# A fifth buffer of probabilities, one output staging tile less, and the exponential listed ahead of the copies in even slots

## The chip, the core and the metric

The kernel runs on one core of a Trainium2 chip. The core has five engines that each work through a queue of their own, in order: TensorE (PE in the profile; its weight loads are shown as PEld), VectorE (DVE), ScalarE (ACT), GpSimd (POOL) and SyncE (SP, which here only issues DMAs). They meet through semaphores. The metric is the time of one execution on the device, in microseconds (us), as the median of several runs.

## What is computed

Four batches of eight attention heads, 768 positions, 64 channels a head. A key counts for a query only if both fall into the same bucket of a hash of six sign bits. The heads of a batch, side by side, are the input of a gated convolution and two matrix products.

```python
def _attn_ref(q, k, v, proj):
    q_bits = (np.einsum('bhsd,dk->bhsk', q, proj) > 0)
    k_bits = (np.einsum('bhsd,dk->bhsk', k, proj) > 0)
    ...
    scores = scale * np.matmul(q, k.transpose(0, 1, 3, 2))
    scores = np.where(mask, scores, -1000000000.0)
    scores = scores - np.max(scores, axis=-1, keepdims=True)
    attn = np.exp(scores)
    attn = attn / (np.sum(attn, axis=-1, keepdims=True) + 1e-09)
    return np.matmul(attn, v)

def _moe_ref(x, w_val, conv_w, w_out):
    ...
    gate = 1.0 / (1.0 + np.exp(-gate_pre))
    val = x @ w_val
    return (gate * val @ w_out)
```

Here `gate_pre` is a causal convolution of five taps along the positions, each channel for itself.

## The kernel before

A **unit** is one head of one batch: 32 units. Each is cut into six query tiles of 128 rows, so there are 192 tiles, and one loop runs over **slots** k, with one tile entering the pipeline per slot. The order of the work on PE, DVE, ACT and POOL is the order of the program text: the schedule is written by hand, and each engine's queue is in order. What a slot k lists, engine by engine:

- **PE**: `scores(k + 1)` (four matrix products, L291, into one of two PSUM tiles `s`), then four matrix products of the feed-forward part (`moe`, L424 or L449) where a batch is ready for it, in odd slots two steps of `attn_v` (L362, into the tile `av`), and at the end `transposes(k - 3)`: six transpositions of 128x128 of the probabilities `p` of tile k-3 (L339), three into each of two PSUM tiles `tp`.
- **ACT**: `keep_transposed(k - 4)`, two copies (L348) that bring the two `tp` tiles of the previous slot's transpositions to SBUF (`pt`), then `exponentials(k)`, one exponential of 128x768 (L315) from `s` into a tile `p`, with the row sum accumulated. After that come, in some slots, an output copy (L457) or the two copies of a finished `av` into `x` (L370). A unit's `attn_v` begins three slots after its last tile and takes three odd slots, so its `x` copies stand at the end of an odd slot, once in every six slots, and the next slot, an even one, follows them in ACT's queue.
- **DVE**: the row maximum `nm` (L297), in even slots the row sums of the tiles k-2 and k-1 (L321), the scale `gs` (L303), in even slots the reciprocals (L325), the bias `nb` (L307) on which the exponential waits; then parts of the convolution (`g`, L393), the gate product `ht` (L429) and roundings.
- **POOL**: `normalise(k - 2)`, which multiplies `p` by the reciprocal (L330), and subtractions that split numbers into two parts.
- **SP**: the loads, the DMAs that rearrange a unit's operands, and the output DMAs (L459).

Four buffers matter for what follows. `s` has two, so `scores(k + 2)` waits for `exponentials(k)`. `tp` has two tiles, so the two halves of `transposes(k - 3)` wait for the two copies of `keep_transposed(k - 4)`. `p` has `LAG + 1 = 4` tiles, so `exponentials(k)` writes the tile from which `transposes(k - 4)`, of slot k-1, has read. The staging tile of an output, `o`, has two.

`outp` ends an output tile of 128x512: accumulated in PSUM, copied to `o` by DVE or ACT, sent out by a DMA on SP's queue. The last slots (k from 192 on) hold no scores, and after the loop the rest of the feed-forward part runs with `cur["end"]` set.

Of the kernel before, what the change touches and what calls it, by code (L numbers as in the profile page):

```python
# [8 lines left out]
FP32 = mybir.dt.float32  # L9
# [17 lines left out]
def kernel(  # L27
# [12 lines left out]
    P = 128  # L40
    D = 64
    KB = S // P
    HS = S // 2
    NP = H // 2
    KW = 5
    LAG = 3
# [5 lines left out]
    raw = ctx.enter_context(tc.tile_pool(name="raw", bufs=5))  # L52
    stk = ctx.enter_context(tc.tile_pool(name="stk", bufs=2))
    vp = ctx.enter_context(tc.tile_pool(name="vp", bufs=2))
    pp = ctx.enter_context(tc.tile_pool(name="pp", bufs=LAG + 1))
    small = ctx.enter_context(tc.tile_pool(name="small", bufs=6))
    ptp = ctx.enter_context(tc.tile_pool(name="ptp", bufs=6))
    xp = ctx.enter_context(tc.tile_pool(name="xp", bufs=2))
# [1 line left out]
    gp = ctx.enter_context(tc.tile_pool(name="gp", bufs=5))  # L60
    hp = ctx.enter_context(tc.tile_pool(name="hp", bufs=5))
    wst = ctx.enter_context(tc.tile_pool(name="wst", bufs=2))
    op = ctx.enter_context(tc.tile_pool(name="op", bufs=2))

    dram = ctx.enter_context(tc.tile_pool(name="dram", bufs=4, space=bass.MemoryType.DRAM))
    ps_s = ctx.enter_context(tc.tile_pool(name="ps_s", bufs=2, space=PSUM))
# [192 lines left out]
    def first_bits():  # L259
        yield from bits(0)  # L260
        load_raw(5)
# [47 lines left out]
    def exponentials(k):  # L309
        s, nb = ss.pop(k), nbs.pop(k)  # L310
        p = pp.tile([P, 2, HS], FP32, name="p")
        if k % 2 == 0:
            cur["sm"] = small.tile([P, 2, 2], FP32, name="sm")
        sm = cur["sm"]
        nc.scalar.activation(out=p, in_=s[:, :, 0:HS], func=AF.Exp, bias=nb, scale=gs.pop(k), accum_out=sm[:, k % 2, 0:1])  # L315
        ps[k] = (p.rearrange("p a b -> p (a b)"), sm)
# [25 lines left out]
    def keep_transposed(k):  # L342
        i, qt = tiles[k]
        if qt % 3 == 0:
            cur["pts"].append([ptp.tile([P, 3, HS], FP32, name="pt") for _ in range(2)])
        qo = (qt % 3) * P
        for pt, tp in zip(cur["pts"][-1], tps.pop(k)):
            nc.scalar.copy(out=pt[:, :, qo:qo + P], in_=tp[:, 0:HS].rearrange("p (a b) -> p a b", b=P))  # L348
        if qt == KB - 1:
            avs.append(attn_v(i, cur["pts"]))  # L350
            cur["pts"] = []

    def attn_v(i, pts):
        b, h = units[i]
        hh, c = h % 2, h // 2
        av = ps_v.tile([P, 512], FP32, name="av")
        vt = vts[i]
        for kb in range(KB):
            if kb:
                yield  # L360
            for s, pt in enumerate(pts):
                nc.tensor.matmul(out=av[s * D:(s + 1) * D, 0:HS], lhsT=vt[:, kb, hh * D:(hh + 1) * D], rhs=pt[kb // 3][:, kb % 3, :],  # L362
                                 start=(kb == 0), stop=(kb == KB - 1), tile_position=(0, s * D))
        if hh == 0:
            x = cur["x"] = xp.tile([P, S + KW - 1], FP32, name="x")
            nc.gpsimd.memset(x[:, 0:KW - 1], 0.0)
        x = cur["x"]
        for s in range(2):
            o = KW - 1 + s * HS
            nc.scalar.copy(out=x[hh * D:(hh + 1) * D, o:o + HS], in_=av[s * D:(s + 1) * D, 0:HS])  # L370
        if hh == 1:
            if c == 0:
                cur["xs"], cur["g"] = {}, []
            convs.append(pair_x(b, c, x, cur["g"], cur["xs"]))
# [34 lines left out]
    def moe(b, xs_, g):  # L409
        hs = {}  # L410
        todo = []

        def later():
            while todo:
                todo.pop(0)()

        def val(o, j):
            acc = acc_tile()
            m = 0
            for wi, xi in ((0, 0), (1, 0), (0, 1)):  # L420
                if m:
                    yield
                for c in range(NP):
                    nc.tensor.matmul(out=acc[:, 0:HS], lhsT=wv[wi][:, c, j * P:(j + 1) * P],  # L424
                                     rhs=xs_[(c, o)][xi], start=(m == 0), stop=(m == 11))
                    m += 1
                later()
            ht = hp.tile([P, HS], FP32, name="ht", bufs=2)
            nc.vector.tensor_tensor(out=ht, in0=acc[:, 0:HS], in1=g[j][:, o:o + HS], op=ALU.mult)  # L429

            def split():
                hh = hp.tile([P, HS], FP32R, name="hh")
                nc.vector.tensor_copy(out=hh, in_=ht)  # L433
                hl = hp.tile([P, HS], FP32R, name="hl")
                nc.gpsimd.tensor_tensor(out=hl, in0=ht, in1=hh.bitcast(FP32), op=ALU.subtract)  # L435
                hs[(o, j)] = (hh, hl)
            todo.append(split)
            yield

        def outp(o, tb):  # L440
            for gens in weights:
                finish(gens)
            acc = acc_tile()
            m = 0
            for hi, wi in ((0, 0), (0, 1), (1, 0)):
                if m:
                    yield
                for j in range(NP):
                    nc.tensor.matmul(out=acc, lhsT=hs[(o, j)][hi][:, tb * P:(tb + 1) * P],  # L449
                                     rhs=wo[wi][:, j, :], start=(m == 0), stop=(m == 11))  # L450
                    m += 1
                later()
            ob = op.tile([P, 512], FP32, name="o")
            if cur["gates"]:
                nc.vector.tensor_copy(out=ob, in_=acc)
            else:
                nc.scalar.copy(out=ob, in_=acc)  # L457
            r0 = o + tb * P
            nc.sync.dma_start(out=out[b, r0:r0 + P, :], in_=ob)  # L459
            yield  # L460

        def idle(n):
            for _ in range(n):
                later()
                yield

        def hold():
            while len(moes) < 2 and not cur["end"]:
                yield

        chunks = [(val, 0, j) for j in range(NP)]
        chunks += [(val, HS, 0)] + [(outp, 0, tb) for tb in range(3)] + [(val, HS, j) for j in range(1, NP)]
        chunks += [(idle, 2)] + [(outp, HS, tb) for tb in range(3)]
        if b < B - 1:
            chunks.insert(-2, (hold,))
        for f, *args in chunks:
            yield from f(*args)
# [5 lines left out]
    raws, stacks, vts, ss, nbs, ps, tps, sums, rcs, nms, gs, cur = {}, {}, {}, {}, {}, {}, {}, {}, {}, {}, {}, {}  # L483
# [11 lines left out]
    def finish(gens):  # L495
        while gens:
            step(gens)

    cur["gates"], cur["end"], cur["pts"] = 0, False, []
    N = len(tiles)  # L500
    with tc.manual_schedule(engines=ENGINES):
        for i in range(5):
            load_raw(i)
        load_values(0)
        first_prep()
        weights = [[load_weights()], [load_conv()]]
        preps = [first_bits(), prep(1)]
        scores(0)
        next(preps[1])
        step(preps)  # L510
        step(weights[0])
        step(weights[1])
        ahead = [early_bits()]
        for k in range(N + LAG + 1):
            if 0 <= k - LAG - 1:
                keep_transposed(k - LAG - 1)
            pair = k % 2 == 0 and 0 <= k - 2 < N
            if k < N:
                maxima(k)
            if pair:  # L520
                row_sums(k - 2)
            if k < N:
                factors(k)
            if pair:
                recip(k - 2)
            if 0 <= k - 2 < N:
                normalise(k - 2)
            if k < N:
                shifts(k)
            if k + 1 < N:  # L530
                if tiles[k + 1][0] != tiles[k][0]:
                    finish(preps)
                    preps = [prep(tiles[k + 1][0] + 1)]
                scores(k + 1)
            if k < N:
                exponentials(k)
            if k >= 60 or k % 2:
                step(convs)
            if k % 6 in (0, 2, 4, 5) and k > 4:
                step(weights[0])  # L540
            elif k < 6:
                step(weights[1])

            thin = k // 6 % 8 in (7, 0) and k < 186
            for _ in range(3 if cur["gates"] else (1, 0)[k % 2] if thin else 1):
                step(moes)
            cur["gates"] = max(0, cur["gates"] - 1)
            step(preps)
            if 6 <= k < 60 and k % 6 in (3, 4):
                step(ahead)  # L550
            if k % 2:
                step(avs)
                step(avs)
            if 0 <= k - LAG < N:
                transposes(k - LAG)
        accs[:] = [(ps_m, "m"), (ps_t, "tp"), (ps_s, "s"), (ps_t, "tp"), (ps_s, "s")]
        finish(avs)
        cur["gates"] = 0
        cur["end"] = True
        while convs:  # L560
            step(convs)
            step(moes)
        finish(moes)
# [59 lines left out]
```

## Time and profile before

| | us |
|---|---|
| median of 3 runs | 621.56 (620.15 to 621.71) |
| the profiled execution, its own time | 621.24 |
| its span, first to last instruction | 619.2 |
| ACT copies of L348, 384 of them | 165.7 |
| POOL busy | 387.6 |
| granted TensorE clock over the span | 0.997 |

The profile is of one execution; its page gives the busy time of every engine, the span in 40 slices, the chain of work that ended last, and the costliest groups of instructions. In a group's row stand the line of the kernel, the engine, the operation, what it writes and reads, how often it ran, its busy time and the mean of one, and then the idle time of the engine just before, with what ended most of it. In a row of the timeline stand the start and the length in us, the engine, the line, the operation, the tiles, and how many instructions are merged in the row; idle time before it is in brackets with its releaser. Matrix products are pipelined: the recorded end of one lies about a quarter of a microsecond behind the start of the next.

### The profile page before, as it was taken

The page shows a single profiled execution, that of the slowest core. Times are in us where ns is not written, and L with a number is a line of the kernel's source. Part 1 is how long each engine was busy: PE and PEld are TensorE (multiplying, and loading weights), DVE is VectorE, ACT ScalarE, POOL GpSimd, SP SyncE. Part 2 cuts the span into 40 slices and gives each one's busy share as a digit, 9 for nine tenths or more (in the row PEclk, how much of TensorE's full clock was granted, in tenths as well). Part 3 has the DMA queues.
Part 4 walks back from the last instruction along what each step waited for, and adds up shares of the span by engine and source line. Part 5 has one row for each costly group of instructions (what it writes and reads, how often), then busy time and mean ns, then how long its engine had stood idle before and what let it go on. Part 6 is the DMA issues. An engine that isn't in the chain of part 4 may idle for free.

```text
span 619.2 us, 10665 instructions
## 1 busy us (share of the span) xinstructions
PE 585.0 (94%) x3496; PEld 421.4 (68%) x3496; DVE 434.5 (70%) x1017; ACT 420.3 (68%) x881; POOL 387.6 (63%) x373
## 2 busy tenths in 40 slices
PE   5799998989899999999999999999999999999997
PEld 2665655556567776776668787777667777775895
DVE  5787889898885866668575867668665877665532
ACT  2786777677778676777787676777787766765400
POOL 3575777677866765578665777468764776544321
PEclk9899999999999999999999999999999999999999
DMA  7575767473533334243434234333422213200111
GB/s 228 167 209 168 216 170 208 129 202 82 132 82 74 79 77 130 73 108 83 125 80 115 55 83 123 87 112 83 108 70 78 68 43 92 66 19 1 51 52 51
DMA packets 29030, 64.64 MB, mean 104 GB/s; under 512 B 4936, under 2 KB 10056, under 8 KB 28976
## 3 DMA queue, kind: packets, MB, share of 16 engines
q1 hardware_dynamic: 28832, 63.93, 37.7%
q8 instruction: 28, 0.46, 0.3%
q14 instruction: 26, 0.21, 0.1%
q10 hardware_dynamic: 144, 0.03, 0.0%
HBM read 30.60 MB, written 7.86 MB: 62 GB/s over the span
## 4 chain that ended last, share of the span: by engine, by line
PE 71%; ACT 14%; DVE 11%; issue 2%; DMA 2%; SPq 0%; POOL 0%; ACTq 0%; DVEq 0%; POOLq 0%
PE av L362 19%; PE s L291 17%; PE tp L339 13%; PE m L449 8%; PE m L424 7%; ACT p L315 6%; ACT pt L348 4%; DVE nm L297 3%; ACT x L370 2%; DVE g L393 2%; PE tp L424 1%; PE tp L449 1%; PE s L449 1%; PE m L229 1%; PE s L424 1%
## 5 line engine op out<-in xcount | busy, mean ns | idle before, releaser
L330 POOL TENSOR_SCALAR p<-p,ri 128x768 f32<-128x768 f32 x192 | 205.0, 1072 | 157.7 <-DVE nb L307 131.3
L297 DVE TENSOR_REDUCE nm<-s 128x1 f32<-128x768 f32 x192 | 182.6, 951 | 63.9 <-PE s L291 63.5
L348 ACT COPY pt<-tp 128x384 f32<-128x384 f32 x384 | 165.7, 485 | 81.7 <-PE tp L339 80.9
L315 ACT ACTIVATE p<-s,nb,gs 128x768 f32<-128x768 f32 x192 | 192.7, 1003 | 40.5 <-DVE nb L307 35.6
L339 PEld LDWEIGHTS tp<-ident,p 128*128 128x128 f32 x1152 | 129.2, 141 | 71.8 <-issue 45.2
L339 PE MATMUL tp<-ident,p 128*128 128x128 f32 x1152 | 163.8, 278 | 2.8 <-ACT pt L348 2.2
L362 PE MATMUL av<-pt,vt 128*64 128x384 f32 x768 | 144.9, 498 | 0.0
L291 PE MATMUL s<-ak,aq 76*128 76x384 f32 x384 | 117.7, 387 | 19.6 <-ACT p L315 16.9
L291 PE MATMUL s<-bk,bq 128*128 128x384 f32 x384 | 100.6, 343 | 0.4 <-DVE bq L277 0.4
L362 PEld LDWEIGHTS av<-pt,vt 128*64 128x64 f32 x768 | 46.9, 136 | 63.0 <-issue 62.9
L291 PEld LDWEIGHTS s<-ak,aq 76*128 76x128 f32 x384 | 59.0, 193 | 35.6 <-ACT p L315 31.8
L393 DVE SCALAR_TENSOR_TENSOR g<-x,cw_sb,g 128x768 f32<-128x768 f32 x64 | 77.3, 1208 | 2.2 <-POOL g L391 2.1
L291 PEld LDWEIGHTS s<-bk,bq 128*128 128x128 f32 x384 | 71.2, 192 | 0.8 <-issue 0.8
L198 POOL TENSOR_TENSOR bq<-r,aq 128x768 fp32r<-128x768 f32 x31 | 57.5, 1853 | 0.1
L435 POOL TENSOR_TENSOR hl<-ht,hh 128x384 fp32r<-128x384 f32 x32 | 32.2, 1006 | 39.4 <-DVE hh L433 39.4
L370 ACT COPY x<-av 64x384 f32<-64x384 f32 x64 | 30.4, 474 | 30.9 <-PE av L362 30.2
L383 POOL TENSOR_TENSOR xl<-x,xh 128x384 fp32r<-128x384 f32 x32 | 33.4, 1059 | 18.0 <-DVE xh L382 18.0
L424 PE MATMUL m<-xh,wv 128*128 128x384 f32 x200 | 42.7, 337 | 0.0
L307 DVE TENSOR_SCALAR nb<-nm,gs 128x1 f32<-128x1 f32 x192 | 40.2, 209 | 3.5
L315 ACT ACTIVATION_READ_ACCUMULATOR p<-s,nb,gs 128x1 f32 x192 | 39.1, 203 | 0.0
L429 DVE TENSOR_TENSOR ht<-m,g 128x384 f32<-128x384 f32 x25 | 13.9, 556 | 35.7 <-PE m L424 29.3
L449 PE MATMUL m<-wo,hh 128*128 128x512 f32 x144 | 38.1, 394 | 0.0
(86 smaller groups left out, 483.7 us busy)
## 6 DMA issues: line engine op xcount, KB each, us to landing
r<-in_qk_dram SPq DMA_DIRECT2D x32, 384.0 KB
vt<-in_v_dram SPq DMA_DIRECT2D x16, 384.0 KB
out_dram<-o SPq DMA_DIRECT2D x24, 256.0 KB
ak<-aq SPq DMA_DIRECT2D x31, 192.0 KB
bk<-aq SPq DMA_DIRECT2D x31, 192.0 KB
bk<-bq SPq DMA_DIRECT2D x31, 192.0 KB
bq<-aq SPq DMA_DIRECT2D x31, 192.0 KB
hh<-in_qk_dram SPq DMA_DIRECT2D x16, 192.0 KB
```

What stands on the lines that cost most here:

```text
L198: nc.gpsimd.tensor_tensor(out=bq, in0=r, in1=aq.bitcast(FP32), op=ALU.subtract)
L291: nc.tensor.matmul(out=s[:, hf, 0:HS], lhsT=lq[0:n, qs], rhs=rk[0:n, hf * HS:(hf + 1) * HS], start=n == M, stop=n == P)
L297: nc.vector.tensor_reduce(out=nm, in_=s[:, :, 0:HS], axis=AX.XY, op=ALU.max, negate=True)
L315: nc.scalar.activation(out=p, in_=s[:, :, 0:HS], func=AF.Exp, bias=nb, scale=gs.pop(k), accum_out=sm[:, k % 2, 0:1])
L330: nc.gpsimd.tensor_scalar(out=p, in0=p, scalar1=rcs.pop(k), scalar2=1.0, op0=ALU.mult, op1=ALU.mult)
L339: nc.tensor.transpose(out=tp[:, n * P:(n + 1) * P], in_=p[:, kb * P:(kb + 1) * P], identity=ident)
L348: nc.scalar.copy(out=pt[:, :, qo:qo + P], in_=tp[:, 0:HS].rearrange("p (a b) -> p a b", b=P))
L362: nc.tensor.matmul(out=av[s * D:(s + 1) * D, 0:HS], lhsT=vt[:, kb, hh * D:(hh + 1) * D], rhs=pt[kb // 3][:, kb % 3, :], start=(kb == 0), s ...
L370: nc.scalar.copy(out=x[hh * D:(hh + 1) * D, o:o + HS], in_=av[s * D:(s + 1) * D, 0:HS])
L393: nc.vector.scalar_tensor_tensor(out=g, in0=x[:, k:k + S], scalar=w, in1=g, op0=ALU.mult, op1=ALU.add)
L424: nc.tensor.matmul(out=acc[:, 0:HS], lhsT=wv[wi][:, c, j * P:(j + 1) * P], rhs=xs_[(c, o)][xi], start=(m == 0), stop=(m == 11))
L449: nc.tensor.matmul(out=acc, lhsT=hs[(o, j)][hi][:, tb * P:(tb + 1) * P], rhs=wo[wi][:, j, :], start=(m == 0), stop=(m == 11))
```

## The change

Three edits. The ring of probabilities gets a fifth buffer. The staging tile `o` has one buffer in place of two, and after the loop the outputs are staged in the ring `p`, which is then free. In even slots below N = 192, `keep_transposed(k - 4)` is no longer listed at the head of the slot but behind `exponentials(k)`; odd slots, and those from 192 on, are as before.

```diff
-    pp = ctx.enter_context(tc.tile_pool(name="pp", bufs=LAG + 1))
+    pp = ctx.enter_context(tc.tile_pool(name="pp", bufs=LAG + 2))
...
-    op = ctx.enter_context(tc.tile_pool(name="op", bufs=2))
+    op = ctx.enter_context(tc.tile_pool(name="op", bufs=1))
...
-            ob = op.tile([P, 512], FP32, name="o")
+            if cur["end"]:
+                ob = pp.tile([P, 2, HS], FP32, name="p").rearrange("p a b -> p (a b)")[:, 0:512]
+            else:
+                ob = op.tile([P, 512], FP32, name="o")
...
         for k in range(N + LAG + 1):
-            if 0 <= k - LAG - 1:
+            if 0 <= k - LAG - 1 and (k % 2 or k >= N):
                 keep_transposed(k - LAG - 1)
...
             if k < N:
                 exponentials(k)
+                if k % 2 == 0 and 0 <= k - LAG - 1:
+                    keep_transposed(k - LAG - 1)
```

## The prediction, made before the change was run

> **What bounds the kernel now.** I read the page's busy times first, then the table of windows, the list of waits and the timeline.
>
> ```profile
> span 619.2 us, 10665 instructions
> PE 585.0 (94%) x3496; PEld 421.4 (68%) x3496; DVE 434.5 (70%) x1017; ACT 420.3 (68%) x881; POOL 387.6 (63%) x373
> PE 71%; ACT 14%; DVE 11%; issue 2%; DMA 2%; SPq 0%; POOL 0%; ACTq 0%; DVEq 0%; POOLq 0%
> ```
>
> PE carries the kernel: 94% busy and 71% of the chain that ended last. The windows (length, then busy time of PE, PEld, DVE, ACT, POOL) show where it isn't full:
>
> ```profile
> 10.10:193.00 182.90, 165.54 (x1026) 106.31 (x1026) 152.78 (x363) 136.37 (x290) 123.06 (x120) 0.99 0.56 155
> 193.00:557.10 364.10, 359.00 (x2166) 267.50 (x2165) 250.73 (x604) 266.32 (x562) 240.82 (x228) 1.00 0.33 85
> ```
>
> From 193 us on, PE idles 364.1 - 359.0 = 5.1 us in all, so nothing that frees another engine can gain more there. Before 193 us it idles 17.4 us, and DVE is busy 84% of that time. The waits name the causes (total, times, longest):
>
> ```profile
> ACT pt L348 <- PE tp L339: 80.9, 96, 2.1
> ACT p L315 <- DVE nb L307: 35.6, 45, 6.0
> PE s L291 <- ACT p L315: 16.9, 34, 2.0
> PE tp L339 <- ACT pt L348: 2.2, 7, 0.8
> ```
>
> ACT waits 80.9 us, 96 times, for transpositions that its next copies need. ACT isn't the bound, so that idle time costs nothing by itself. What costs is PE waiting for an exponential that frees an s tile: 16.9 us. That, with the 2.2 us for copies, is all that an order of ACT's queue could win.
>
> **The change part by part.** The reorder comes first. In an even slot ACT had the two copies, then the exponential; now the exponential, then the copies. No instruction is added. ACT's queue issues no DMA here, and neither SP's nor POOL's queue is moved past. But PE needs both: the copies free the tp tiles for the next transpositions, the exponential frees the s tile for the scores after these. The transpositions are listed first, so the copies are needed first.
>
> Slot A, behind x copies (one in six slots), with ACT's rows, PE's, the weight load of the scores and the bias:
>
> ```profile
> 409.27 0.97 ACT L370 COPY x<-av 64x384 f32<-64x384 f32 x2 [0.64 <-PE av L362]
> 410.27 0.86 ACT L348 COPY pt<-tp 128x384 f32<-128x384 f32 x2
> 411.02 1.01 ACT L315 ACTIVATE p<-s,nb,gs 128x768 f32<-128x768 f32 x1
> ```
>
> ```profile
> 409.15 0.87 PE L339 MATMUL tp<-ident,p 128*128 128x128 f32 x6
> ...
> 411.26 0.81 PE L339 MATMUL tp<-ident,p 128*128 128x128 f32 x6
> 412.17 0.62 PE L291 MATMUL s<-ak,aq 76*128 76x384 f32 x2
> ```
>
> ```profile
> 412.17 0.30 PEld L291 LDWEIGHTS s<-ak,aq 76*128 76x128 f32 x2 [0.33 <-ACT p L315]
> ```
>
> ```profile
> 409.00 0.21 DVE L307 TENSOR_SCALAR nb<-nm,gs 128x1 f32<-128x1 f32 x1
> ```
>
> The bias is there at 409.21, the x copies hold ACT until 410.24. Copies at 410.27, exponential at 411.02, transpositions at 411.26 without a stall, scores at 412.17 after a weight-load wait of 0.33 for the exponential. With the order turned I need three steps from rows elsewhere: how soon copies follow an exponential, a stalled transposition its copy, and scores their transpositions. Another x slot, in which PE had no feed-forward work:
>
> ```profile
> 458.50 0.86 ACT L348 COPY pt<-tp 128x384 f32<-128x384 f32 x2
> 459.24 1.01 ACT L315 ACTIVATE p<-s,nb,gs 128x768 f32<-128x768 f32 x1
> ...
> 460.23 0.48 ACT L348 COPY pt<-tp 128x384 f32<-128x384 f32 x1
> ```
>
> ```profile
> 459.12 0.85 PE L339 MATMUL tp<-ident,p 128*128 128x128 f32 x6
> ```
>
> Exponential to copies: 460.23 - 459.24 = 0.99. Copies to stalled transpositions: 459.12 - 458.50 = 0.62. So in slot A: exponential at 410.27, copies 411.26, transpositions 411.88 in place of 411.26, their end 0.85 later, 412.73. Scores may start 0.25 before that recorded end (slot B below: 352.25 + 0.82 against 352.82), at 412.48 in place of 412.17. The stall for the exponential goes, and a longer one for the copies takes its place: **0.3 us lost**.
>
> Slot B, without x copies but with a late bias (PE's rows, then the bias, then the next bias and its exponential):
>
> ```profile
> 350.12 0.88 PE L339 MATMUL tp<-ident,p 128*128 128x128 f32 x6
> ...
> 352.25 0.82 PE L339 MATMUL tp<-ident,p 128*128 128x128 f32 x6
> 352.82 0.60 PE L291 MATMUL s<-ak,aq 76*128 76x384 f32 x2
> ```
>
> ```profile
> 351.02 0.19 DVE L307 TENSOR_SCALAR nb<-nm,gs 128x1 f32<-128x1 f32 x1
> ```
>
> ```profile
> 353.55 0.21 DVE L307 TENSOR_SCALAR nb<-nm,gs 128x1 f32<-128x1 f32 x1
> ```
>
> ```profile
> 353.86 0.99 ACT L315 ACTIVATE p<-s,nb,gs 128x768 f32<-128x768 f32 x1 [0.22 <-DVE nb L307]
> ```
>
> Bias end to exponential is 353.86 - 353.76 = 0.10. The bias of slot B ends at 351.21, so the exponential starts at 351.31, copies 352.30, transpositions 352.92, end 353.77, scores 353.52: **0.70 us later** than 352.82, where PE had no wait before. This is an added wait: the copies are queued behind an exponential that waits for DVE, the transpositions wait for the copies, and behind these stand the next scores, since PE's queue is in order.
>
> The general rule from these steps: scores come 0.99 + 0.62 + 0.85 - 0.25 = 2.21 us after the exponential's start. Where neither x copies nor bias hold the exponential past about 0.45 us after the start of the transpositions, that is no later than before (2.7 us), and nothing is lost or won.
>
> I applied this to the 93 even slots from k = 4 to 188, each against the scores' start in the trace. 30 follow x copies. In 28 of them the turn costs at least 0.30: **8.4 us**, firm (in the other two PE waits longer for something else). In nine of them the bias comes later still, 4.1 us more. Of the 63 others, 32 lose by a late bias, 17.8 us in all; the first and the last:
>
> ```profile
> 22.25 0.21 DVE L307 TENSOR_SCALAR nb<-nm,gs 128x1 f32<-128x1 f32 x1
> ```
>
> ```profile
> 491.62 0.19 DVE L307 TENSOR_SCALAR nb<-nm,gs 128x1 f32<-128x1 f32 x1
> ```
>
> So the late biases sum to 21.9 us, but not all is paid. Two slots after B the bias is late again, because DVE has worked without a pause since before B:
>
> ```profile
> 357.40 0.21 DVE L307 TENSOR_SCALAR nb<-nm,gs 128x1 f32<-128x1 f32 x1
> ```
>
> That slot was counted at 0.77 beyond its x copies. If slot B has already put PE back 0.70, DVE has caught up and the 0.77 nearly vanishes. A run of late slots pays about once, and before 193 us, where most late slots lie (13.2 of the 17.8), DVE is nearly the bound. Where the bias is late because a gate product waited for PE, the loss stays. Bounds: 0 (all absorbed) and 21.9 (none). The nearest rows are those of B and its follower, where 0.70 of 0.70 + 0.77 is paid, 48%; I take half, **11.0 us**.
>
> The fifth p buffer costs no time: ACT's copies already waited for the transpositions that release the fourth, so it alone frees nothing; it is what lets the exponential go first. One staging tile: the next output copy must wait for the DMA. The closest pair in the loop, and the last output:
>
> ```profile
> 324.26 0.36 SPq L459 DMA_DIRECT2D out_dram<-o  x1
> ```
>
> ```profile
> 329.26 0.69 DVE L455 COPY o<-m 128x512 f32<-128x512 f32 x1 [3.72 <-PE m L449]
> ```
>
> ```profile
> 613.28 3.08 SPq L459 DMA_DIRECT2D out_dram<-o  x2
> ```
>
> 5.0 us lie between issue and next copy. The second of the last two is issued at about 616.0 (613.28 + 3.08 less 0.3), and the span ends 3.2 us later, landing included. So the wait has passed. If a landing took twice 3.2 us, two such pairs would cost 1.4 us each; at the other end nothing, and no gain, since nothing waited. I take 0. After the loop outputs follow every 2.75 us; two tiles sufficed (5.5 against 3.2), so a ring of five wins nothing.
>
> Sum: 8.4 + 11.0 = 19.4 us, none of it hidden, as PE is the bound. Against the profiled execution's own 621.24 us (span 619.2, 2.0 around it; 0.3 below the median of 621.56) that gives **640.6 us**.
>
> **The rivals.**
>
> *Only the x slots pay.* DVE catches up everywhere: 621.2 + 8.4 = 629.6. For it: DVE's idle time elsewhere. Against: biases that are late behind a gate product move with PE.
>
> *Everything pays.* 621.2 + 8.4 + 21.9 = 651.5. For it: odd exponentials also start later (their copies follow the delayed transpositions), so row sums and the next bias can be late again. Against: the run after slot B.
>
> *The other side, faster: the copies come in time.* The place is the even slot's second transposition, the price the 16.9 us that PE now waits for exponentials. It decides when the exponential starts within 0.45 us of the transpositions' start. Then the wait goes and nothing replaces it: 604.3, or 612.8 if half. Slot A speaks against it, as x copies end at +1.1 us.
> [...]
>
> *No difference*: losses and regained waits cancel, 621.2.
>
> **How the numbers follow.** Forecast (640.6, give or take 6) 0.43; x slots alone 0.27; everything 0.15; faster 0.09; no difference 0.06. The range reaches from 626, a little under the x slots alone, to 653, a little over everything, which leaves out the last two and some tails. Slower by over 0.3% (1.9 us, about what a measurement can tell from no change): 0.43 + 0.27 + 0.15 = 0.85, plus 0.01 of the undecided case; same 0.05; faster 0.09.
>
> **What would show it.** PE's wait for ACT's copies (2.2 us now) should grow to 15 us or more, in even slots, and its wait for exponentials (16.9) should fall below 10. ACT's wait for transpositions (80.9) should shrink, and more exponentials should wait for the bias. In an x slot the order is x copies, exponential, copies, then stalled transpositions. Staging shows no wait before an output copy. The prediction fails if the transpositions don't stall in x slots, if DVE absorbs more than half, or if the waits for exponentials that vanish were worth more than the rows say.

## The result: 3.5% slower

The changed kernel takes 643.13 us (median of 5 runs, 641.36 to 643.94), the kernel before 621.52 (5 runs, 620.15 to 621.71): a ratio of 1.0351, 95% interval 1.0331 to 1.0370. The forecast was 640.6 in a range of 626 to 653.

The page of the changed kernel's profiled execution (its own time 643.23 us), the lines that answer to those of before; in a group's row, the numbers behind the last bar are idle time before it and what ended it:

```profile
span 641.0 us, 10614 instructions
PE 585.0 (91%) x3496; PEld 419.9 (65%) x3496; DVE 433.7 (68%) x1017; ACT 423.3 (66%) x881; POOL 384.6 (60%) x373
PE 64%; DVE 15%; ACT 11%; DMA 3%; issue 3%; POOL 3%; SPq 0%; ACTq 0%; POOLq 0%; DVEq 0%
...
L339 PE MATMUL tp<-ident,p 128*128 128x128 f32 x1152 | 166.1, 281 | 40.2 <-ACT pt L348 34.9
```

PE is busy the same 585.0 us, in a span that is 21.8 us longer. Its share of the chain that ended last went from 71% to 64%, DVE's from 11% to 15%. The idle time before the transpositions is new. The list of waits of the same execution (total, times, longest) says for whom:

```profile
ACT p L315 <- DVE nb L307: 67.1, 80, 6.0
ACT pt L348 <- PE tp L339: 44.7, 99, 1.4
PE tp L339 <- ACT pt L348: 34.9, 47, 2.0
PE s L291 <- ACT p L315: 2.6, 3, 2.0
```

Two waits have changed places. PE waits for exponentials 2.6 us in place of 16.9, as the change meant, and for copies 34.9 us in place of 2.2. ACT's wait for transpositions, which looked like the thing to win, did shrink: 44.7 us, where there were 80.9. But ACT's idle time wasn't won by it: its wait for the bias grew from 35.6 to 67.1 us, and over the whole span ACT idles 217.7 us (641.0 - 423.3), where it idled 198.9 (619.2 - 420.3).

Slot A (behind x copies) and slot B (late bias) in the changed kernel, for each ACT's rows and then PE's rows of the timeline:

```profile
427.42 0.97 ACT L370 COPY x<-av 64x384 f32<-64x384 f32 x2 [0.64 <-PE av L362]
428.42 0.99 ACT L315 ACTIVATE p<-s,nb,gs 128x768 f32<-128x768 f32 x1
429.31 0.19 ACT L315 ACTIVATION_READ_ACCUMULATOR p<-s,nb,gs 128x1 f32 x1
429.40 0.85 ACT L348 COPY pt<-tp 128x384 f32<-128x384 f32 x2
```

```profile
427.31 0.87 PE L339 MATMUL tp<-ident,p 128*128 128x128 f32 x6
...
430.01 0.84 PE L339 MATMUL tp<-ident,p 128*128 128x128 f32 x6 [0.43 <-ACT pt L348]
430.61 0.59 PE L291 MATMUL s<-ak,aq 76*128 76x384 f32 x2
```

```profile
367.86 1.00 ACT L315 ACTIVATE p<-s,nb,gs 128x768 f32<-128x768 f32 x1 [1.56 <-DVE nb L307]
...
368.85 0.85 ACT L348 COPY pt<-tp 128x384 f32<-128x384 f32 x2
```

```profile
366.66 0.88 PE L339 MATMUL tp<-ident,p 128*128 128x128 f32 x6
...
369.46 0.85 PE L339 MATMUL tp<-ident,p 128*128 128x128 f32 x6 [0.52 <-ACT pt L348]
370.06 0.42 PE L291 MATMUL s<-ak,aq 76*128 76x384 f32 x1
```

In A the exponential now starts at once behind the x copies, the copies 0.98 us later, the second transpositions 0.61 us behind them after a stall, and the scores come 430.61 - 427.31 = 3.30 us after the first transpositions: 3.02 before (412.17 - 409.15), and 3.33 in the working. In B it is 370.06 - 366.66 = 3.40: 2.70 before, 3.40 in the working.

### The profile page after: what moved, and what is told of

Its sections match the earlier page's. It is cut to its first block, busy times and chain, and to the rows that moved or that the text cites. A ratio compares the mean times of both kernels' runs of the same rounds, so it can differ in the third digit from the quotient of the medians.

```text
span 641.0 us, 10614 instructions
## 1 busy us (share of the span) xinstructions
PE 585.0 (91%) x3496; PEld 419.9 (65%) x3496; DVE 433.7 (68%) x1017; ACT 423.3 (66%) x881; POOL 384.6 (60%) x373
## 4 chain that ended last, share of the span: by engine, by line
PE 64%; DVE 15%; ACT 11%; DMA 3%; issue 3%; POOL 3%; SPq 0%; ACTq 0%; POOLq 0%; DVEq 0%
PE av L362 16%; PE tp L339 15%; PE s L291 14%; PE m L449 7%; ACT p L315 7%; PE m L424 6%; DVE nm L297 5%; DVE g L393 4%; ACT pt L348 2%; ACT x L370 2%; POOL p L330 2%; PE tp L424 1%; PE tp L449 1%; PE s L449 1%; DMA bk<-bq 1%
## 5 line engine op out<-in xcount | busy, mean ns | idle before, releaser
L330 POOL TENSOR_SCALAR p<-p,ri 128x768 f32<-128x768 f32 x192 | 202.2, 1057 | 175.8 <-DVE nb L307 165.9
L315 ACT ACTIVATE p<-s,nb,gs 128x768 f32<-128x768 f32 x192 | 191.3, 996 | 87.1 <-DVE nb L307 67.1
L339 PEld LDWEIGHTS tp<-ident,p 128*128 128x128 f32 x1152 | 126.7, 142 | 120.8 <-issue 63.9
L339 PE MATMUL tp<-ident,p 128*128 128x128 f32 x1152 | 166.1, 281 | 40.2 <-ACT pt L348 34.9
L348 ACT COPY pt<-tp 128x384 f32<-128x384 f32 x384 | 164.6, 481 | 44.8 <-PE tp L339 44.7
L362 PE MATMUL av<-pt,vt 128*64 128x384 f32 x768 | 147.0, 504 | 0.0
L393 DVE SCALAR_TENSOR_TENSOR g<-x,cw_sb,g 128x768 f32<-128x768 f32 x64 | 77.4, 1209 | 2.2 <-POOL g L391 2.1
L429 DVE TENSOR_TENSOR ht<-m,g 128x384 f32<-128x384 f32 x25 | 13.9, 556 | 41.1 <-PE m L424 33.8
L315 ACT ACTIVATION_READ_ACCUMULATOR p<-s,nb,gs 128x1 f32 x192 | 37.7, 196 | 0.0
```

Source lines behind the costliest of these rows:

```text
L330: nc.gpsimd.tensor_scalar(out=p, in0=p, scalar1=rcs.pop(k), scalar2=1.0, op0=ALU.mult, op1=ALU.mult)
L339: nc.tensor.transpose(out=tp[:, n * P:(n + 1) * P], in_=p[:, kb * P:(kb + 1) * P], identity=ident)
L393: nc.vector.scalar_tensor_tensor(out=g, in0=x[:, k:k + S], scalar=w, in1=g, op0=ALU.mult, op1=ALU.add)
```

## The experiments

Most runs turn the order (exponential ahead of the copies) in chosen slots only, with the buffers of the changed kernel:

```diff
+            turned = k < N and CONDITION
-            if 0 <= k - LAG - 1 and (k % 2 or k >= N):
+            if 0 <= k - LAG - 1 and not turned:
...
-                if k % 2 == 0 and 0 <= k - LAG - 1:
+                if turned and 0 <= k - LAG - 1:
```

Medians, each beside the kernel before on the same chip:

| run | turned slots, other edits | us | ratio (95% interval) |
|---|---|---|---|
| changed kernel | all even | 643.13 | 1.0351 (1.0331 to 1.0370) |
| e1 | none | 621.70 | 1.0007 (0.9995 to 1.0018) |
| e2 | all even, four p tiles | 655.60 | 1.0562 (1.0531 to 1.0593) |
| e3 | the 30 behind x copies | 635.19 | 1.0236 (1.0219 to 1.0253) |
| e4 | all other even ones | 634.07 | 1.0225 (1.0203 to 1.0248) |
| e5 | 31 with an early bias | 621.75 | 1.0014 (1.0001 to 1.0028) |
| e6 | 32 with a late bias | 634.61 | 1.0224 (1.0201 to 1.0247) |
| e7 | none, buffers as before, x copies later | 632.10 | 1.0181 (1.0160 to 1.0203) |
| e8 | all even, x copies later | 649.32 | 1.0475 (1.0439 to 1.0510) |
| e9 | as e7, roundings of x later too | 617.81 | 0.9950 (0.9931 to 0.9969) |
| e10 | all even, PE's stalls filled | 641.90 | 1.0334 (1.0315 to 1.0352) |

### e1: the buffers without the order

`CONDITION` is `False`.

> Five probability tiles, one staging tile, outputs staged in the ring after the loop, but the copies ahead of the exponential in every slot, as before. If the order alone costs (my theory), 621.5 us, within 1.9. If the single staging tile or the place of the tiles in memory costs, anything above 624, up to the 643 of the changed kernel.

621.70 us. The fifth tile, the single staging tile and the staging in the ring after the loop cost nothing and bring nothing; the rival that put the loss on staging falls. The whole loss is the order.

### e2: the order without the fifth buffer

```diff
-    pp = ctx.enter_context(tc.tile_pool(name="pp", bufs=LAG + 2))
+    pp = ctx.enter_context(tc.tile_pool(name="pp", bufs=LAG + 1))
```

> The changed kernel with four probability tiles again. The exponential of an even slot then waits for the end of the transpositions that read its tile, about 0.9 us after their start, and the copies stand behind it. Theory (the copies behind the exponential are what PE waits for): nearly every even slot without x copies has its scores at 0.95 + 2.21 = 3.16 us in place of 2.7, so 643 plus up to 31 times 0.4 = 12 us more: 650 to 657 us. Rival (the fifth tile is of no account, the order alone does it): 643 us.

655.60 us, as the theory said. ACT's row, then PE's rows, of an even slot without x copies and with an early bias, in e2's timeline:

```profile
429.66 0.99 ACT L315 ACTIVATE p<-s,nb,gs 128x768 f32<-128x768 f32 x1 [2.10 <-PE tp L339]
```

```profile
428.70 0.88 PE L339 MATMUL tp<-ident,p 128*128 128x128 f32 x6
...
431.85 0.60 PE L291 MATMUL s<-ak,aq 76*128 76x384 f32 x2
```

The exponential waits for the transpositions that read its tile and starts 429.66 - 428.70 = 0.96 us after their start. The scores come at 3.15 us; the working said 3.16. So the fifth tile does what it is for: with the order turned it is worth 655.6 - 643.1 = 12.5 us. Without the turned order it is worth nothing (e1).

### e3 and e4: behind x copies, and the rest

`CONDITION` is `k % 6 == 2 and k >= 14` in e3, and `k % 2 == 0 and (k % 6 != 2 or k < 14)` in e4.

> The order is turned in the 30 even slots behind x copies alone; all other slots as before, buffers as in the changed kernel. Theory: 8.4 us for the x copies and up to 4.1 for late biases there: 630 to 634 us. Rival (late biases do all of it): 622 us.

> The order is turned in all even slots but the 30 behind x copies. Theory: the late biases, 11 of 17.8 us paid: 630 to 635 us. If both sums are additive, this and the run before lie 21.6 us above 621.5 when added. Rival (only x copies cost): 622 us.

e3 costs 14.2 us (635.19 - 620.97), just above its range; e4 costs 13.1, within. Neither rival holds: both kinds of slot pay. Together they lose 27.3 us, the changed kernel 21.6, so they are not additive. That fits the catching-up of DVE that the prediction reasoned with. The slot that follows B by two shows it. PE's rows and the bias, first in the kernel before, then in e3, then in the changed kernel:

```profile
355.84 0.88 PE L339 MATMUL tp<-ident,p 128*128 128x128 f32 x6
...
358.85 0.62 PE L291 MATMUL s<-ak,aq 76*128 76x384 f32 x2
```

```profile
364.51 0.88 PE L339 MATMUL tp<-ident,p 128*128 128x128 f32 x6
...
367.99 0.85 PE L339 MATMUL tp<-ident,p 128*128 128x128 f32 x6 [1.20 <-ACT pt L348]
368.59 0.60 PE L291 MATMUL s<-ak,aq 76*128 76x384 f32 x2
```

```profile
366.08 0.21 DVE L307 TENSOR_SCALAR nb<-nm,gs 128x1 f32<-128x1 f32 x1
```

```profile
373.08 0.87 PE L339 MATMUL tp<-ident,p 128*128 128x128 f32 x6
...
375.85 0.84 PE L339 MATMUL tp<-ident,p 128*128 128x128 f32 x6 [0.49 <-ACT pt L348]
376.45 0.60 PE L291 MATMUL s<-ak,aq 76*128 76x384 f32 x2
```

```profile
373.95 0.21 DVE L307 TENSOR_SCALAR nb<-nm,gs 128x1 f32<-128x1 f32 x1
```

Before, scores came 3.01 us after the transpositions. In e3, where slot B isn't turned, they come at 4.08: the bias ends 1.78 us after the transpositions' start, and the full 0.30 + 0.77 is paid. In the changed kernel slot B has put PE back 0.70, the bias ends at 1.08, and the scores come at 3.37: 0.36 is paid. Of the 0.70 + 0.77 beyond the x copies, the two slots pay 0.76.

### e5 and e6: early bias, late bias

The 63 even slots without x copies, split by the working of the prediction: `CONDITION` is `k in` a list of 31 slots without a loss (e5), or of 32 with one (e6).

> The order is turned in the 31 even slots alone for which the working found no loss: no x copies ahead, and the bias early enough that scores come no later. Theory: 621.5 us, within 2. Rival (a turned slot costs whatever stands around it, about 21.6 / 93 = 0.23 us each): 628.7 us.

> The order is turned in the 32 even slots without x copies alone whose bias comes late. Theory: the same as turning all slots without x copies, 630 to 635 us, and at most 621.5 + 17.8 = 639.3. Rival (each turned slot costs 0.23 us): 628.9 us.

e5 loses about 1.1 us (621.75 against 620.67; by its interval between 0.1 and 1.7), where an even charge on each turned slot would have been 7.1. e6 costs about as much as e4 (13.9 and 13.1 us). So a turned slot costs by what stands around it: little or nothing where the exponential is ready early, and in the other 32 slots all that the slots without x copies lose.

### e7, e8 and e9: the x copies one slot later

If the x copies hold both the copies and the exponential, they can go behind them. In e7 and e8 the two copies of `attn_v` are kept in a list and issued behind the next slot's exponential (and, in e8, its copies); the diff is shortened:

```diff
-        for s in range(2):
-            nc.scalar.copy(out=x[...], in_=av[...])
-        if hh == 1:
-            convs.append(pair_x(b, c, x, cur["g"], cur["xs"]))
+        cur["xc"].append(copies)          # the same lines, as a function
...
             if k < N:
                 exponentials(k)
+            while cur["xc"]:
+                cur["xc"].pop(0)()
             if k >= 60 or k % 2:
                 step(convs)
```

> The kernel before, with one thing moved: the two x copies of a finished unit stand one slot later, behind that slot's exponential, and no longer ahead of its copies. Theory (x copies hold both copies and exponential, and PE waits for the exponential): most of the 7.5 us that PE waits for exponentials in the slots behind x copies goes: 614 to 618 us. Rival (the x copies are needed by DVE, whose roundings then come late and hold the next row maximum): 621 us or above.

> The changed kernel with the x copies one slot later, behind that slot's exponential and copies. Theory: in slots behind x copies the exponential then waits only for its bias, so about the 8.4 us of these slots comes back: 632 to 636 us. Rival (the loss isn't tied to the x copies): 643 us.

Both are misses: 632.10 and 649.32 us. e7's rival was right. Rows of e7's timeline, DVE, ACT and PE:

```profile
416.83 1.66 DVE L386 CAST xh<-x 128x384 fp32r<-128x384 f32 x2 [2.89 <-ACT x L372]
...
418.88 0.94 DVE L297 TENSOR_REDUCE nm<-s 128x1 f32<-128x768 f32 x1
...
420.05 0.21 DVE L307 TENSOR_SCALAR nb<-nm,gs 128x1 f32<-128x1 f32 x1
...
420.36 0.99 ACT L315 ACTIVATE p<-s,nb,gs 128x768 f32<-128x768 f32 x1 [2.17 <-DVE nb L307]
...
421.49 0.62 PE L291 MATMUL s<-ak,aq 76*128 76x384 f32 x2 [1.32 <-ACT p L315]
```

DVE stands idle 2.89 us in front of a rounding of x that waits for the late copies. Behind it in DVE's queue stands the next row maximum, so the bias is late, ACT waits 2.17 us for it, and PE 1.32 us for the exponential. It is the same fault as in the change under study, on another engine: an instruction that isn't ready stands ahead of one that is needed sooner. In e7 the slots behind x copies gained 7.0 us and the slots right after them lost 14.2 (the intervals from one tile's scores to the next, summed over the kind of slot, against the kernel before; the expectation of e9 puts these at 13.4). In e8 the same sums show the same load on top of the change: against the kernel before, the slots behind x copies are 2.8 us shorter, but the slots right after them 11.2 us longer and the next ones 11.4.

e9 is e7 with the list of pairs extended only behind `step(convs)`, so that the roundings are listed one step later.

> The kernel before with the two x copies one slot later, behind that slot's exponential, and DVE's roundings of x one step later too, behind the next bias, so that they no longer wait in front of a row maximum. Theory (the run with the x copies alone moved lost because the roundings held DVE until the late copies; 13.4 us came in the slots after): the x slots keep their gain of about 7 us and the 13.4 us go: 614 to 618 us. Rival (a later x delays the whole convolution chain and so the gates): 621 us or above.

617.81 us, within the theory's range, at its upper end: 0.5% faster than the kernel before (0.9931 to 0.9969), and the fastest version here. By the same sums the slots behind x copies gained 10.3 us and the slots right after them 0.7, but the ones two and three slots after them gave 7.1 back. The wait list still shows 16.6 us of PE waiting for exponentials; the wait for copies is gone from it.

### e10 and e11: the clock

The changed kernel's profile has stretches in which the granted TensorE clock is 0.5. e10 fills PE's stalls in 22 even slots with transpositions of the identity into columns of the score tile that nobody reads; e11 is the changed kernel unedited, for a second profile.

```diff
+            for n in range(FILL.get(k, 0)):
+                nc.tensor.transpose(out=ss[k + 1][:, 0, HS:512], in_=ident, identity=ident)
             if 0 <= k - LAG < N:
                 transposes(k - LAG)
```

> The changed kernel with transpositions of the identity put into the stalls of 22 even slots, 4 to 13 each, sized to the stall that the trace shows there, into columns of the score tile that nobody reads. The profile of the changed kernel has four stretches of 3.4 us with the granted clock at 0.5, the kernel before one. Theory (PE's idle time in those stalls brings the clock down, at up to 1.7 us a stretch): fewer such stretches and 638 to 641 us. Rival (the lowered clock costs nothing, as PE waits there anyway): 643 us. If the row maximum is held up by the added work, the time rises above 645, and only the count of stretches tells.

> The changed kernel once more, for a second profile. If the stretches of lowered clock at 166.6 and 303.2 us belong to the stalls at these places, they come again there. Rival (they fall by chance on one of several places): other places, or another count, and the span then differs from 641.0 by about 1.6 us for each stretch more or less.

e10 takes 641.90 us, between the two theories. The waits for copies fell from 34.9 to 21.5 us, since the fill stands in their place, and the time hardly changed (1.0334 against 1.0351, with intervals that overlap): what bounds the slot is the late copy, not PE's idleness. The records of the granted clock hold four stretches again, as the changed kernel's do (19.9, 30.1, 166.6 and 303.2 us), but all before 39 us, none at 166.6 or 303.2: the granted clock was 1.00 from 162.6 to 170.0 and from 303.0 to 307.0 us. In e11, one execution of 641.18 us with a span of 639.0, there are three, at 27.6, 95.8 and 300.6 us (granted clock 0.96 from 10 to 100 us, 1.00 from 100 to 300, 0.98 from 300 to 400). So the stretch near 300 came twice, the one at 166.6 did not come again, and one stretch less goes with a span 2.0 us shorter.

How much of the loss is the clock's can be bounded by the mean granted clock of every timed execution: 0.984 to 0.989 in the five of the changed kernel, 0.993 to 1.000 in the 37 of the kernel before that ran beside e1 to e11. A mean of 0.984 over 641.8 us is 2 x 0.016 x 641.8 = 20.5 us at half rate, or six stretches of 3.4 us. On average it is 4.9 stretches in the changed kernel and 1.5 in the kernel before. At 1.6 us for each, as measured in the last section, the 3.4 more are worth at most 5.4 of the 21.6 us (an estimate: a stretch in which PE waits anyway costs less). The rest, 16 us or more, is the order's without the clock.

## Why the prediction was right

**The order costs, the buffers don't.** Right: e1 for the buffers, e3 and e4 for the order. The staging tile shows no wait; in the changed kernel's timeline the second of the closest pair of outputs still waits for PE alone:

```profile
345.52 0.69 DVE L458 COPY o<-m 128x512 f32<-128x512 f32 x1 [3.72 <-PE m L449]
```

**The three steps of a turned slot** (0.99, 0.62, 0.60 to the scores) held to 0.05 us in A, B and the slot of e2, although the trace of before holds no turned slot.

**The x slots, 8.4 us, and the late biases, 11.0 of 21.9.** Over the same 93 even slots, by the sums of intervals from one tile's scores to the next, the changed kernel's intervals are 19.4 us longer than those before: 8.6 in the 30 slots behind x copies and 10.8 in the 63 others (8.3 and 11.3 in the second profile). The sum of the two terms was 19.4.

The 8.4 is right slot by slot: most x slots paid 0.29 or 0.30 us. That the half taken for the late biases came out to 0.2 us is in part luck. It was one pair's share, and it is made up of unequal ones: of the 4.1 us in the x slots about 0.2 was paid, of the 17.8 in the 32 others 11.2, and the 31 early slots gave 0.3 back. The reason given, that a run of late slots pays about once, shows in neighbours: 0.60 and 0.56 us were worked out for the slots 22 and 24, and 0.60 and -0.03 paid; 1.08 each for 30 and 34, and 1.15 and -0.14 paid. That DVE absorbs more where it is nearly the bound is hardly shown: 8.2 of 13.2 us were paid before 193 us, 3.2 of 4.6 after it. And with one kind of slot turned alone more is paid: 13.1 of the 17.8 in e6.

e3, without the other even slots turned, paid 14.2 where 8.4 + 4.1 were worked out. By the same sums its x slots paid 13.7, the odd slots 2.2, and the other even slots gave 1.6 back. Of the x slots two paid too much, slots 98 and 110: 1.20 and 1.23 where 0.61 and 0.55 were worked out. In both, the convolution step on DVE ahead of the row maximum (L393) took longer than before, 1.47 us for 1.03 and 2.17 for 1.83, which makes the bias later; that covers 0.44 + 0.34 of the 1.27, and the rest is open. Right behind these two stand the stretches of lowered clock of its profile, at 292.3 and 326.4 us (its mean granted clock was 0.992). They lie in the odd slots 99 and 111, which grew by 1.39 and 1.34 us.

**Nothing hidden, no gain.** Right. The waits for exponentials fell to 2.6 us, below the 10 that were named, and the waits for copies rose above the 15. ACT's exponentials waited for the bias 80 times in place of 45, as was said. Of the rivals, "only the x slots pay" falls by e6, "everything pays" by the slot after B, and "faster" by slot A.

**What was not in the sum** is the difference of 2.2 us to the measured 21.6. The odd slots grew by 1.9 us, which the working had at nothing. In two of them, 55 and 99, lie stretches of lowered clock (0.50 from 166.6 and from 303.2 us, next section but one); these two grew by 1.41 and 1.56 us, and the other odd slots gave 1.1 back. The clock is a term that the prediction doesn't have.

## What to carry to other kernels

Idle time on an engine that isn't the bound is no reserve: ACT's 80.9 us of waiting for transpositions shrank by nearly half, its waiting for the bias grew by almost as much, and the kernel got slower. In an in-order queue, put first what the bounding engine needs first, and see in its own queue which result that engine needs first; here the copies came before the exponential. Before a move, ask also what the moved instruction itself waits for, since from then on everything behind it waits for that too (the bias here, the x copies in e7).

## What the runs showed of the hardware

In the changed kernel the granted clock fell to 0.50 in stretches of 3.4 us in the middle of the run, not only near its start. Windows of the changed kernel's execution (length, busy time of PE, PEld, DVE, ACT, POOL with the number of instructions, then the granted clock, the DMA share and GB/s):

```profile
162.60:166.60 4.00, 2.02 (x16) 1.69 (x15) 3.93 (x10) 2.22 (x6) 3.37 (x3) 1.00 0.40 87
166.60:170.00 3.40, 3.40 (x14) 2.15 (x15) 2.76 (x6) 1.94 (x4) 2.15 (x2) 0.50 0.53 102
...
303.20:306.60 3.40, 3.40 (x12) 1.33 (x12) 1.40 (x5) 2.05 (x4) 2.40 (x3) 0.50 0.00 0
```

Each follows a stall of nearly 2 us. These rows of PE's timeline stand ahead of the first and of the second stretch, the last one in the kernel before:

```profile
166.19 1.11 PE L339 MATMUL tp<-ident,p 128*128 128x128 f32 x6 [1.98 <-ACT pt L348]
```

```profile
301.77 0.85 PE L339 MATMUL tp<-ident,p 128*128 128x128 f32 x6 [1.81 <-ACT pt L348]
...
303.27 2.83 PE L362 MATMUL av<-pt,vt 128*64 128x384 f32 x8
```

```profile
289.34 1.51 PE L362 MATMUL av<-pt,vt 128*64 128x384 f32 x8
```

The eight products took 2.83 us, where they took 1.51 before. With the transpositions behind them, 1.12 for 0.87, that one stretch cost about 1.3 + 0.25 = 1.6 us, so a stall that such a stretch follows is paid a second time.

The changed kernel's four stretches, at 19.9, 30.1, 166.6 and 303.2 us, begin 3, 40 and 40 times 3.413 us apart ((303.2 - 19.9) / 83 = 3.413), e11's three 20 and 60 times. The same stall was followed by a stretch in one execution and not in the other. The changed kernel stalls for 1.98 us before 166.19, and e11 for 1.99 before 165.59; only the first is followed by a stretch, and e11's granted clock from 160 to 172 us was 1.00. Counted in steps of 3.413 us from the stretches of its own execution, the two stalls lie in these 3.40 us (e11's but for its first 0.5), the changed kernel's first and then e11's:

```profile
163.20:166.60 3.40, 1.42 (x11) 1.12 (x10) 3.33 (x9) 1.83 (x4) 2.77 (x3) 1.00 0.47 103
```

```profile
164.10:167.50 3.40, 1.91 (x14) 1.50 (x16) 3.33 (x5) 3.08 (x7) 3.40 (x3) 1.00 0.56 123
```

PE is busy 1.42 of 3.40 us, 42%, in the one, and 1.91, 56%, in the other. In the 3.41 us ahead of each of the changed kernel's four stretches, PE is busy 1.12, 1.89, 1.43 and 1.60 us: 33, 55, 42 and 47%. In the 3.41 us from 129.08 it is busy 1.74 us, 51%, and the clock behind them was 1.00. So the length of the stall alone doesn't tell the two executions apart. Nor does PE's busy share part all of these cases: 55% had a stretch behind it, 51% and 56% had none. e2, with a span of 652.7 us, 11.7 longer than the changed kernel's, had a mean granted clock of 0.992, where the changed kernel had 0.989.
